# Packed attention and two MLPs: another order and pace for the weight conversions of the first batch

## The chip, the cores and the metric

The kernel runs on one core of a Trainium2 chip. The core's engines each take their own instructions strictly in order and wait for one another through semaphores: PE (TensorE: matrix products and transposes), DVE (VectorE), ACT (ScalarE), POOL (GpSimd) and SP (SyncE, which here only issues transfers between DRAM and on-chip memory). PEld in the profile is PE's loading of weights. The metric is the device time of one execution in microseconds (us); less is better.

## The reference, cut to what matters

For 8 batches of 576 tokens with 8 heads of 64, packed attention is followed by two MLPs on 4608 tokens of 512 features, with 2048 hidden features:

```python
def sm_attn(qq, kk, vv):                    # softmax attention, scale 1/sqrt(64)
    ...
p_packed = sm_attn(p, k, v)                 # 32 packed queries a head
out = sm_attn(q, p_packed, p_packed)
x = out.transpose(0, 2, 1, 3).reshape(B * S, H * D)
h = x @ moe_w_in;  g = h - tanh(h);  x = g @ moe_w_out            # first MLP
h = x @ moe2_w_in; g = s * relu(h) ** 2 + b; out = g @ moe2_w_out  # second MLP
```

The four weight matrices arrive as 64-bit floats; q, k, v and p as 32-bit floats.

## The kernel before, in words

Two stages follow each other. The first goes through the batches and makes attention and the first MLP together; the second makes the second MLP from the result, which lies in DRAM (x2t). Only the start of the first stage is changed.

**Conversion.** `to_f32` makes a 32-bit float of the two 32-bit words of each 64-bit number, in five steps: the absolute value of the high word on ACT (line 118), a clamp (L120), a shift with a mask (L122) and two bitwise merges (L125, L128), the last four on DVE. w_in1 is converted in four quarters of columns, `("w1", c, i)` being half i of quarter c (tiles `w1s_c_i`, result `w1_c`). w_out1 is converted in 16 tiles of 128 rows (`wo1s_j`); each is then split into a high and a low part, `wo[j]`, by ACT (L137) and POOL (L139), since each product is made as three products of such parts.

**The first MLP.** The attention's second product and w_in1 are merged: for each batch and quarter, `make_z` multiplies the packed values with `w1[c]` (`zp`, L364) and splits the result into `z` (L429 on ACT, L431 on DVE). A tile j of 128 hidden features of half a batch (288 tokens, `hf`) is then `mm1` (six products into `h`, L450), `act1` (tanh on ACT, L458; h minus tanh on DVE, L459), `split_g` (`gh` on ACT, L133; `gl` on POOL in batch 0, L134) and, two or three tiles later, `mm2` (twelve products into four banks `acc`, L473). Only two banks hold an `h`, so the third tile's `mm1` waits until the first has passed L459.

**Batch 0** has four parts of eight tiles: both halves with tiles 0 to 7, and then both with tiles 8 to 15 (`part[0]` counts them). Tiles 0 to 7 need quarters 0 and 1 and tiles 0 to 7 of w_out1, tiles 8 to 15 the others. At the end of a part the banks `acc` are emptied into `xs` (L97 on ACT, L99 on DVE) and stored to x2t (L491); the third and fourth part load this back (L496) and add it (L485).

**What sets the order.** The program is written out by hand through generators. `fill` is a list of steps beside the tiles: the conversions and the attention of this and the next batch. In batch 0 `AFTER[part]` steps are put behind each `mm1`, and `SLOTS[part]` sixths of a step at each of a tile's six slots; `until(key, fill)` forces as many as a product still needs. Within `first_weights`, `in_turn` takes groups one after the other, the members of a group by turns (`both`), and gives each member of the next group its first step early. `CATCH_UP` steps follow each `mm1` once the weights are done, until the first half of batch 1 has its attention. Each engine then runs what this leaves in its queue.

**Places.** Half quarters of w_in1 are loaded into nine slots, in the order of `turns`. The 64-bit tiles 0 to 7 of w_out1 lie in places of `wo` that are filled last; tiles 8 to 11 and 13 can only be loaded when POOL has split one of those, tile 12 lies in `cv`. All these loads, the store of `xs` and the loads of q, k, v and p (L168, L175, L176, L226, L237) are in SP's one queue, in program order.

Of the kernel before, what the change touches and what calls it, by code (L numbers as in the profile page):

```python
# [18 lines left out]
def pack_attention_two_mlps(ctx, tc, q, k, v, p, w_in1, w_out1, w_in2, w_out2, s_in, b_in, out):  # L19
# [33 lines left out]
    LAND = 14  # L53
    W_K, W_P, W_PK, W_PV, W_E, W_Q = 2, 9, 5, 1, 7, 3

    AFTER, SLOTS = (3, 4, 1, 1), (0, 1, 4, 1)
    AHEAD, CATCH_UP, FIRST_W = 13, 11, (23, 25, 26, 27, 28)
    EXP_LO, EXP_HI = 2.0 ** -15, 2.0 ** 16 * 1.875
    assert 2 * R == P and NB == 2 * C and 4 * M == P and 2 * D == P and H * D == DM

# [460 lines left out]
    def run(g):  # L521
        for _ in g:
            pass

    with tc.manual_schedule():
# [72 lines left out]
        def second_stage(b, hf):  # L598
            yield from scores2(b, hf)
            yield from both([stage2(b, hf, g) for g in range(G)])  # L600
            done.add(("a", b, hf))

        def in_turn(*groups):

            groups = [[call_late(g) for g in group] for group in groups]
            for n, group in enumerate(groups):
                for i, _ in enumerate(both(group)):
                    yield
                    if i == min(AHEAD, 4 * len(group)) and n + 1 < len(groups):
                        for g in groups[n + 1]:  # L610
                            next(g)

        def call_late(f):
            g, *a = f
            yield from g(*a)
# [14 lines left out]
        v_t[0, 0] = v_t[0, 1] = first_rows(v[0], P, v_0, flat(wslot(F32, "v_0_1")))  # L630
        q_t[0, 0] = first_rows(q[0, :, :HB], QT, wo_place(4), odd[:, :DM])
        take_turn()
        load_wo1(0, 1)
        q_t[0, 1] = first_rows(q[0, :, HB:], QT, wo_place(6), wo_place(7))
        load_wo1(2, 3)
        take_turn()
        take_turn()
        load_wo1(4, 5, 6, 7)
        make_identity(nc, ident)
        nc.vector.memset(mask, 0.0)  # L640
        nc.vector.memset(ones, 1.0)
# [11 lines left out]
                next(conv, None)  # L653
        free(len(own) + 1)
        run(conv)
        rest = in_turn([(wo1_steps, 0), (wo1_steps, 1)], [(wo1_steps, 2), (wo1_steps, 3)])
        run(both([second_stage(0, 0), first_z(0), seq(wait(10), turn_q(1))]))
        nc.sync.dma_start(out=s_sb, in_=s_in.partition_broadcast(P))
        nc.sync.dma_start(out=b_sb, in_=b_in.partition_broadcast(P))

        def first_weights():
            yield from rest
            yield from in_turn(
                [(w1_steps, 1, 0), (w1_steps, 1, 1)],
                [(first_z, 1), (wo1_steps, 4), (wo1_steps, 5), (second_stage, 0, 1)],
                [(wo1_steps, 6), (wo1_steps, 7)],
                [(w1_steps, 2, 0), (w1_steps, 2, 1)],
                [(first_z, 2), (wo1_steps, 8), (wo1_steps, 9)],
                [(wo1_steps, 10), (wo1_steps, 11)],
                [(w1_steps, 3, 0), (w1_steps, 3, 1)],  # L670
                [(first_z, 3), (wo1_steps, 12), (wo1_steps, 13)],
                [(wo1_steps, 14), (wo1_steps, 15)])

        pend = []

# [74 lines left out]
        def attention():  # L750

            yield from first_weights()
            load_p(1)
            load_k(1, 0)
            load_v(1, 0)
            for b in range(B):
                if b:
                    for c in range(2, NCH):
                        yield from make_zs(b, c)
                    yield from second_stage(b, 1)  # L760
                if b + 1 == B:
                    return
                load_q(b + 1, 0)
                if b + 2 < B:
                    load_p(b + 2)
                nxt = (b + 2, 0) if b + 2 < B else None
                yield from step_p(b + 1)
                yield from stage1(b + 1, 0, (b + 1, 1), (b + 1, 1))
                yield from stage1(b + 1, 1, nxt, nxt)
                if b:  # L770
                    for c in range(2):
                        yield from make_zs(b + 1, c)
                    yield from second_stage(b + 1, 0)
                else:
                    yield from both([seq(make_zs(1, 0), make_zs(1, 1)), second_stage(1, 0)])
                load_q(b + 1, 1)
# [501 lines left out]
```

## Time and profile before

| | |
|---|---|
| median of 3 runs | 1574.1 us (1573.82 to 1574.97) |
| profiled execution | 1574.41 us |
| its span, first to last instruction | 1572.3 us |
| PE busy | 1485.0 us, 94% of the span |
| DVE busy | 1087.2 us, 69% |
| ACT busy | 745.7 us, 47% |
| POOL busy | 114.5 us, 7% |
| mean granted TensorE clock | 0.973 |

A share of busy time is a mean over stages with different limits, so the stretches of the first 210 us are to be looked at by themselves. The granted clock is 1.0 at the higher of two levels (2.4 GHz) and 0.5 at the lower (1.2 GHz); a stretch with both lies between. A wait in a row is put down to the instruction that ended it last.

### The profile page before, as it was taken

How to read it: one execution, taken by the hardware profiler on the slowest of the kernel's cores; microseconds unless marked ns; L12 is line 12 of the kernel's file. 1: busy time of each engine (PE TensorE's matmuls, PEld its weight loads, DVE VectorE, ACT ScalarE, POOL GpSimd, SP SyncE). 2: the span in 40 equal slices, each digit the busy share in tenths (PEclk: the TensorE clock that was granted, in tenths of full speed). 3: DMA queues.
4: the chain of work that ended last, by engine and by line, in shares of the span. 5: the costliest groups of instructions: out<-in, count | busy, mean ns of one | idle time of the engine just before them, and what ended most of it. 6: DMA issues, size and time to landing. Idle time of an engine off the chain costs nothing.

```text
span 1572.3 us, 27031 instructions
## 1 busy us (share of the span) xinstructions
PE 1485.0 (94%) x10020; PEld 1392.0 (89%) x10020; DVE 1087.2 (69%) x2074; ACT 745.7 (47%) x1433; POOL 114.5 (7%) x143
## 2 busy tenths in 40 slices
PE   5576899999999999999999999999998999999998
PEld 3365688888889889989999999999998999999998
DVE  5777686868769687786744677677676865566563
ACT  3343344444444444443433566566566664454452
POOL 0324200000000010101102000000022000000000
PEclk8588999999999999999999999999999999999999
DMA  9544736464554626352524664664679886686683
GB/s 234 146 115 106 144 82 152 114 151 112 126 139 113 150 77 146 89 132 79 170 82 183 238 251 171 232 240 180 233 270 332 270 255 195 209 254 190 210 243 81
DMA packets 373652, 271.02 MB, mean 172 GB/s; under 512 B 238096, under 2 KB 321040, under 8 KB 373520
## 3 DMA queue, kind: packets, MB, share of 16 engines
q1 hardware_dynamic: 366720, 246.69, 53.2%
q0 software_dynamic: 6272, 22.02, 4.0%
q8 instruction: 78, 1.28, 0.3%
q10 hardware_dynamic: 528, 0.59, 0.1%
q14 instruction: 54, 0.44, 0.1%
HBM read 161.09 MB, written 108.13 MB: 171 GB/s over the span
## 4 chain that ended last, share of the span: by engine, by line
PE 78%; DVE 9%; DMA 4%; SPq 3%; issue 3%; ACT 2%; POOL 0%; ACTq 0%; DVEq 0%; POOLq 0%
PE acc L473 19%; PE Y L1216 10%; PE h L450 9%; PE Y L999 9%; PE Z L1216 6%; PE X L999 6%; PE X L1216 6%; PE Z L999 6%; PE zp L364 2%; DMA w1s<-in_moe_w_in_dram 2%; PE pv L338 1%; PE s L268 1%; SPq L192 1%; DVE gl L134 1%; DVE t L459 1%
## 5 line engine op out<-in xcount | busy, mean ns | idle before, releaser
L473 PE MATMUL acc<-gh,wo 128*128 128x288 f32 x2040 | 422.9, 298 | 1.3 <-POOL wo L139 1.3
L473 PEld LDWEIGHTS acc<-gh,wo 128*128 128x128 f32 x2040 | 333.5, 191 | 1.9 <-POOL wo L139 1.9
L473 PE MATMUL acc<-gl,wo 128*128 128x288 f32 x1020 | 314.6, 308 | 11.8 <-POOL gl L134 8.2
L458 ACT ACTIVATE t<-h 128x288 f32<-128x288 f32 x256 | 105.1, 411 | 333.7 <-PE h L450 287.3
L473 PEld LDWEIGHTS acc<-gl,wo 128*128 128x128 f32 x1020 | 194.5, 191 | 51.7 <-issue 37.2
L459 DVE TENSOR_TENSOR t<-h,t 128x288 f32<-128x288 f32 x256 | 116.2, 454 | 177.6 <-ACT t L458 176.5
L450 PE MATMUL h<-a2h,z 128*128 128x288 f32 x1024 | 216.5, 299 | 3.7 <-DVE z L431 3.7
L903 DVE TENSOR_TENSOR x<-B,x 128x768 fp32r<-128x768 f32 x158 | 147.3, 951 | 80.1 <-ACT x L1150 67.1
L450 PEld LDWEIGHTS h<-a2h,z 128*128 128x128 f32 x1024 | 167.5, 192 | 4.2 <-DVE z L431 4.2
L999 PE MATMUL Y<-x,w 128*128 128x384 f32 x864 | 160.6, 339 | 4.8 <-DVE g L903 4.0
L450 PE MATMUL h<-a2l,z 128*128 128x288 f32 x512 | 155.6, 304 | 7.5 <-DVE a2l L415 6.4
L999 PEld LDWEIGHTS Y<-x,w 128*128 128x128 f32 x864 | 152.9, 190 | 5.4 <-DVE g L903 4.4
L1216 PE MATMUL Y<-x,w 128*128 128x384 f32 x864 | 153.2, 335 | 0.7 <-DVE s L903 0.7
L1216 PEld LDWEIGHTS Y<-x,w 128*128 128x128 f32 x864 | 150.3, 188 | 1.0 <-DVE s L903 1.0
L1150 ACT CAST x<-B 128x768 fp32r<-128x768 f32 x116 | 94.1, 834 | 45.0 <-DMA B<-g 24.4
L450 PEld LDWEIGHTS h<-a2l,z 128*128 128x128 f32 x512 | 98.7, 193 | 13.1 <-DVE a2l L415 7.0
L133 ACT CAST gh<-t 128x288 fp32r<-128x288 f32 x255 | 108.6, 426 | 0.0
L999 PE MATMUL X<-x,w 128*128 128x384 f32 x576 | 108.0, 336 | 0.0
L999 PE MATMUL Z<-x,w 128*128 128x384 f32 x576 | 107.9, 336 | 0.0
L134 DVE TENSOR_TENSOR gl<-t,gh 128x288 fp32r<-128x288 f32 x224 | 104.0, 464 | 0.0
L1216 PE MATMUL X<-x,w 128*128 128x384 f32 x576 | 102.9, 337 | 0.0
L1216 PE MATMUL Z<-x,w 128*128 128x384 f32 x576 | 102.0, 335 | 0.0
(164 smaller groups left out, 2061.7 us busy)
## 6 DMA issues: line engine op xcount, KB each, us to landing
g<-g SPq DMA_DIRECT2D x196, 384.0 KB, 3.6
B<-g SPq DMA_DIRECT2D x116, 384.0 KB, 4.6
w<-w_d POOLq DMA_DIRECT2D x28, 512.0 KB, 5.3
B<-x2t SPq DMA_DIRECT2D x24, 384.0 KB, 5.8
g<-s SPq DMA_DIRECT2D x24, 384.0 KB, 2.9
out_dram<-g SPq DMA_DIRECT2D x192, 48.0 KB, 1.8
x2t<-xs SPq DMA_DIRECT2D x15, 576.0 KB, 3.5
w1s<-in_moe_w_in_dram SPq DMA_DIRECT2D x32, 256.0 KB, 8.0
```

The lines of the kernel that those rows point to most:

```text
L133: nc.scalar.copy(hi, x)
L134: (eng or nc.vector).tensor_tensor(out=lo, in0=x, in1=hi.bitcast(F32), op=ALU.subtract)
L192: nc.sync.dma_start(out=t.rearrange("p (h d) -> p h d", h=H), in_=src[:, t0:t0 + m].rearrange("h p d -> p h d"))
L364: nc.tensor.matmul(ps[e][i * M:(i + 1) * M, :rhs(i).shape[-1]], pblk[b][r, h // 4, h % 4 * M:h % 4 * M + M], rhs(i)[r], start=True, stop=True)
L450: nc.tensor.matmul(h[:, :HB], zt[:, zi, g, f0:f0 + P], a[:, g], start=(n == 0), stop=(n == 3 * G - 1))
L458: nc.scalar.activation(t, h[:, :HB], AF.Tanh)
L459: nc.vector.tensor_tensor(out=t, in0=h[:, :HB], in1=t, op=ALU.subtract)
L473: nc.tensor.matmul(acc[m][:, :HB], w[:, m * P:(m + 1) * P], x, start=(j == js[0] and i == 0), stop=(j == js[-1] and i == 2))
L903: self.nc.vector.tensor_tensor(out=o, in0=a, in1=b, op=op)
L999: self.nc.tensor.matmul(bank[:, f, :self.TH], w[:, f, a, kt], x[:, b, kt], start=(p in ("P1", "P5", "P6") and m == 0), stop=(m == 5), skip ...
L1150: self.nc.scalar.copy(self.xs[(7 * self.NBK + n) % self.XS][:, 0], self.ready[0])
L1216: nc.tensor.matmul(bank[:, ft, :T], w[:, kk, u, ft], x[:, v, kk], start=first and p in ("P1", "P5", "P6"), stop=last, skip_group_check=True)
```

## The change

The order of the groups in `first_weights` is new. Each quarter of w_in1 is converted one half after the other, as two groups of their own, with one or two groups of w_out1 tiles behind them, before the group that holds its product `first_z`; the groups that stood ahead of it (`rest`) are gone. The pace is new: AFTER and SLOTS are (6, 5, 4, 1) and (5, 3, 4, 1) instead of (3, 4, 1, 1) and (0, 1, 4, 1), CATCH_UP is 4 instead of 11. The loads of w_out1 tiles 0 to 7 stand together behind both halves of the second quarter of w_in1 and q's second half. The first loads of batch 1 (`second_loads`) are now part of a group in `first_weights` instead of following all of it.

```diff
@@ -53,8 +53,8 @@
     LAND = 14
     W_K, W_P, W_PK, W_PV, W_E, W_Q = 2, 9, 5, 1, 7, 3
 
-    AFTER, SLOTS = (3, 4, 1, 1), (0, 1, 4, 1)
-    AHEAD, CATCH_UP, FIRST_W = 13, 11, (23, 25, 26, 27, 28)
+    AFTER, SLOTS = (6, 5, 4, 1), (5, 3, 4, 1)
+    AHEAD, CATCH_UP, FIRST_W = 13, 4, (23, 25, 26, 27, 28)
     EXP_LO, EXP_HI = 2.0 ** -15, 2.0 ** 16 * 1.875
     assert 2 * R == P and NB == 2 * C and 4 * M == P and 2 * D == P and H * D == DM
 
@@ -600,6 +600,11 @@
             yield from both([stage2(b, hf, g) for g in range(G)])
             done.add(("a", b, hf))
 
+        def second_loads():
+            for f, *a in ((load_p, 1), (load_k, 1, 0), (load_v, 1, 0), (load_q, 1, 0)):
+                f(*a)
+                yield
+
         def in_turn(*groups):
 
             groups = [[call_late(g) for g in group] for group in groups]
@@ -630,12 +635,10 @@
         v_t[0, 0] = v_t[0, 1] = first_rows(v[0], P, v_0, flat(wslot(F32, "v_0_1")))
         q_t[0, 0] = first_rows(q[0, :, :HB], QT, wo_place(4), odd[:, :DM])
         take_turn()
-        load_wo1(0, 1)
         q_t[0, 1] = first_rows(q[0, :, HB:], QT, wo_place(6), wo_place(7))
-        load_wo1(2, 3)
         take_turn()
         take_turn()
-        load_wo1(4, 5, 6, 7)
+        load_wo1(0, 1, 2, 3, 4, 5, 6, 7)
         make_identity(nc, ident)
         nc.vector.memset(mask, 0.0)
         nc.vector.memset(ones, 1.0)
@@ -653,23 +656,23 @@
                 next(conv, None)
         free(len(own) + 1)
         run(conv)
-        rest = in_turn([(wo1_steps, 0), (wo1_steps, 1)], [(wo1_steps, 2), (wo1_steps, 3)])
         run(both([second_stage(0, 0), first_z(0), seq(wait(10), turn_q(1))]))
         nc.sync.dma_start(out=s_sb, in_=s_in.partition_broadcast(P))
         nc.sync.dma_start(out=b_sb, in_=b_in.partition_broadcast(P))
 
         def first_weights():
-            yield from rest
             yield from in_turn(
-                [(w1_steps, 1, 0), (w1_steps, 1, 1)],
-                [(first_z, 1), (wo1_steps, 4), (wo1_steps, 5), (second_stage, 0, 1)],
-                [(wo1_steps, 6), (wo1_steps, 7)],
-                [(w1_steps, 2, 0), (w1_steps, 2, 1)],
-                [(first_z, 2), (wo1_steps, 8), (wo1_steps, 9)],
-                [(wo1_steps, 10), (wo1_steps, 11)],
-                [(w1_steps, 3, 0), (w1_steps, 3, 1)],
-                [(first_z, 3), (wo1_steps, 12), (wo1_steps, 13)],
-                [(wo1_steps, 14), (wo1_steps, 15)])
+                [(w1_steps, 1, 0)], [(w1_steps, 1, 1)],
+                [(wo1_steps, 0), (wo1_steps, 1)],
+                [(first_z, 1), (wo1_steps, 2), (wo1_steps, 3)],
+                [(wo1_steps, 4), (wo1_steps, 5)],
+                [(second_stage, 0, 1), (wo1_steps, 6), (wo1_steps, 7)],
+                [(w1_steps, 2, 0)], [(w1_steps, 2, 1)],
+                [(wo1_steps, 8), (wo1_steps, 9)],
+                [(first_z, 2), (wo1_steps, 10), (wo1_steps, 11), (second_loads,)],
+                [(w1_steps, 3, 0)], [(w1_steps, 3, 1)],
+                [(wo1_steps, 12), (wo1_steps, 13)],
+                [(first_z, 3), (wo1_steps, 14), (wo1_steps, 15)])
 
         pend = []
 
@@ -750,9 +753,6 @@
         def attention():
 
             yield from first_weights()
-            load_p(1)
-            load_k(1, 0)
-            load_v(1, 0)
             for b in range(B):
                 if b:
                     for c in range(2, NCH):
@@ -760,7 +760,8 @@
                     yield from second_stage(b, 1)
                 if b + 1 == B:
                     return
-                load_q(b + 1, 0)
+                if b:
+                    load_q(b + 1, 0)
                 if b + 2 < B:
                     load_p(b + 2)
                 nxt = (b + 2, 0) if b + 2 < B else None
```

In the rows of the built program below, `t_0_9` is the `t` of half 0, tile 9 (a last number is the buffer's); a `t` of 128x512 with no such numbers is a w_out1 tile under conversion.

First place: DVE, at the first two tiles of the first part. Before, from the first L459 on:

```order
L459 TENSOR_TENSOR t_0_0_482<-h_0_0_470,t_0_0_482 128x288
L120 TENSOR_SCALAR t_479<-t_479 128x512
L122 TENSOR_SCALAR t_477<-t_477 128x512
L122 TENSOR_SCALAR t_479<-t_479 128x512
L459 TENSOR_TENSOR t_0_1_495<-h_0_1_485,t_0_1_495 128x288
L125 SCALAR_TENSOR_TENSOR t_477<-wo1s_174,t_477 128x512
L125 SCALAR_TENSOR_TENSOR t_479<-wo1s_176,t_479 128x512
```

and now:

```order
L122 TENSOR_SCALAR w_1_179<-w_1_179 128x1024
L125 SCALAR_TENSOR_TENSOR w_1_179<-w1s_0_180,w_1_179 128x1024
L128 SCALAR_TENSOR_TENSOR w_1_179<-w1s_0_180,w_1_179 128x1024
L120 TENSOR_SCALAR w_1_179<-w_1_179 128x1024
L459 TENSOR_TENSOR t_0_0_484<-h_0_0_470,t_0_0_484 128x288
L122 TENSOR_SCALAR w_1_179<-w_1_179 128x1024
L125 SCALAR_TENSOR_TENSOR w_1_179<-w1s_1_185,w_1_179 128x1024
L128 SCALAR_TENSOR_TENSOR w_1_179<-w1s_1_185,w_1_179 128x1024
L120 TENSOR_SCALAR t_497<-t_497 128x512
L120 TENSOR_SCALAR t_499<-t_499 128x512
L122 TENSOR_SCALAR t_497<-t_497 128x512
L459 TENSOR_TENSOR t_0_1_504<-h_0_1_488,t_0_1_504 128x288
```

The second quarter (`w_1`) has moved from behind four w_out1 tiles to ahead of all of them, and there are more conversion rows to each L459.

Second place: DVE, where the conversions end (`wo1s_1176` before and `wo1s_1092` now hold tiles 14 and 15 of w_out1). Before:

```order
L459 TENSOR_TENSOR t_0_13_1291<-h_0_13_1282,t_0_13_1291 128x288
L128 SCALAR_TENSOR_TENSOR wo1s_1176<-wo1s_1176,t_1240 128x512
L125 SCALAR_TENSOR_TENSOR t_1266<-wo1s_1176,t_1266 128x512
L128 SCALAR_TENSOR_TENSOR wo1s_1176<-wo1s_1176,t_1266 128x512
L459 TENSOR_TENSOR t_0_14_1323<-h_0_14_1314,t_0_14_1323 128x288
```

and now:

```order
L459 TENSOR_TENSOR t_0_8_1185<-h_0_8_1173,t_0_8_1185 128x288
L122 TENSOR_SCALAR t_1167<-t_1167 128x512
L128 SCALAR_TENSOR_TENSOR wo1s_1092<-wo1s_1092,t_1167 128x512
L125 SCALAR_TENSOR_TENSOR t_1167<-wo1s_1092,t_1167 128x512
L431 TENSOR_TENSOR z_3_1130<-zp_3_1_1132,z_3_1130 128x512
L128 SCALAR_TENSOR_TENSOR wo1s_1092<-wo1s_1092,t_1167 128x512
L459 TENSOR_TENSOR t_0_9_1220<-h_0_9_1207,t_0_9_1220 128x288
```

The last conversion has moved from the L459 of tile 14 to that of tile 9 of the third part.

Third place: SP's queue, from the last of w_out1 tiles 8 to 11 on (`w1s_0`, `w1s_1` are the two halves of the fourth quarter, `cv` is w_out1 tile 12, the row behind it tile 13, the L550 row tiles 14 and 15). Before:

```order
L568 DMA wo1s_813<-in_moe_w_out_dram 128x512
L491 DMA x2t<-xs_0_859 512x1x288
L147 DMA w1s_0_875<-in_moe_w_in_dram 32x2x512 x4
L147 DMA w1s_1_880<-in_moe_w_in_dram 32x2x512 x4
L568 DMA cv<-in_moe_w_out_dram 128x512
L568 DMA wo1s_1115<-in_moe_w_out_dram 128x512
L491 DMA x2t<-xs_1_1152 512x1x288
L496 DMA xp_0_1158<-x2t 128x4x288
L550 DMA wo1s_1176<-in_moe_w_out_dram 128x2x512
L226 DMA pc_1342<-in_p_dram 128x2x64
L168 DMA k_0_0_1344<-in_k_dram 32x18x32 x4
L168 DMA k_0_1_1349<-in_k_dram 32x18x32 x4
```

and now:

```order
L147 DMA w1s_0_812<-in_moe_w_in_dram 32x2x512 x4
L147 DMA w1s_1_852<-in_moe_w_in_dram 32x2x512 x4
L491 DMA x2t<-xs_0_884 512x1x288
L226 DMA pc_914<-in_p_dram 128x2x64
L168 DMA k_0_0_941<-in_k_dram 32x18x32 x4
L168 DMA k_0_1_946<-in_k_dram 32x18x32 x4
L175 DMA v_0_961<-in_v_dram 64x4x320
L176 DMA v_0_961<-in_v_dram 64x4x256
L237 DMA q_0_0_0_986<-in_q_dram 32x9x32 x4
...
L568 DMA cv<-in_moe_w_out_dram 128x512
L568 DMA wo1s_1051<-in_moe_w_out_dram 128x512
L550 DMA wo1s_1092<-in_moe_w_out_dram 128x2x512
```

The fourth quarter has moved ahead of the store of the first part, and batch 1's first loads ahead of w_out1 tile 12.

## Rows read from the trace of the kernel before

**Rows 1.** The page, span in 40 slices: PE's busy tenths, and its granted clock.

```profile
PE   5576899999999999999999999999998999999998
...
PEclk8588999999999999999999999999999999999999
```

**Rows 2.** Busy time by stretch: us, engines (x instructions), PEclk, DMA share, GB/s.

```profile
core 0: us, PE busy (x) PEld busy (x) DVE busy (x) ACT busy (x) POOL busy (x), PEclk, DMA share, GB/s
39.20:161.40 122.20, 77.41 (x459) 65.28 (x459) 91.45 (x140) 47.17 (x96) 44.21 (x37) 0.76 0.48 121
161.40:210.10 48.70, 43.37 (x361) 32.58 (x360) 32.94 (x86) 19.29 (x58) 9.76 (x12) 1.00 0.56 112
```

**Rows 3.** PE's waits, 39.2 to 161.4 us: total us, times, longest us.

```profile
PE zp L364 <- DVE w L128: 19.9, 3, 10.2
```

**Rows 4.** The same stretch, DVE alone, one query each: L120, L122, L125, L128.

```profile
39.20:161.40 122.20, 15.49 (x22) 0.76 0.48 121
...
39.20:161.40 122.20, 17.29 (x22) 0.76 0.48 121
...
39.20:161.40 122.20, 21.43 (x22) 0.76 0.48 121
...
39.20:161.40 122.20, 20.56 (x22) 0.76 0.48 121
```

**Rows 5.** DVE's waits, 39.2 to 161.4 us.

```profile
DVE t L459 <- ACT t L458: 23.1, 10, 4.6
...
DVE w L128 <- PE zp L364: 2.1, 1, 2.1
```

**Rows 6.** Timeline of DVE, last conversion: start us, us, form, idle before.

```profile
159.70 1.69 DVE L128 SCALAR_TENSOR_TENSOR wo1s<-wo1s,t 128x512 int32<-128x512 int32 x1
161.31 0.45 DVE L459 TENSOR_TENSOR t<-h,t 128x288 f32<-128x288 f32 x1
```

**Rows 7.** Chain that ended last, one tile in the first part: start us, us.

```profile
81.39 0.79 PE h L450 x6
82.18 1.61 PE acc L473 x12
```

**Rows 8.** DVE's groups, 39.2 to 161.4 us: busy us, mean ns, idle before.

```profile
L459 DVE TENSOR_TENSOR t<-h,t 128x288 f32<-128x288 f32 x23 | 10.4, 452 | 23.2 <-ACT t L458 23.1
...
L99 DVE COPY xs<-acc 128x288 f32<-128x288 f32 x4 | 1.6, 444 | 0.0
```

**Rows 9.** Tile wo1s, 39.2 to 161.4 us: ns minimum/median/maximum, first and last start.

```profile
L125 DVE SCALAR_TENSOR_TENSOR t<-wo1s,t x15: 676/684/1301, 43.3 to 158.4; 128x512 int32<-128x512 int32 x15
...
L139 POOL TENSOR_TENSOR wo<-wo1s,wo x14: 1287/1482/1841, 47.1 to 159.2; 128x512 fp32r<-128x512 f32 x14
...
DMA to landing us min/median/max: 3.4/3.7/10.2
```

**Rows 10.** Timeline of DVE, conversion rows without POOL beside them.

```profile
41.83 0.42 DVE L120 TENSOR_SCALAR t<-t 128x512 f32<-128x512 f32 x1
...
96.37 0.69 DVE L120 TENSOR_SCALAR w<-w 128x1024 f32<-128x1024 f32 x1 [0.18 <-ACT w L118]
...
99.29 1.21 DVE L125 SCALAR_TENSOR_TENSOR w<-w1s,w 128x1024 int32<-128x1024 int32 x1
```

**Rows 11.** Tile gl, 39.2 to 161.4 us.

```profile
L134 POOL TENSOR_TENSOR gl<-t,gh x22: 794/1037/1359, 43.3 to 160.8; 128x288 fp32r<-128x288 f32 x22
```

**Rows 12.** Timeline of DVE, three of the ten waits of L459.

```profile
80.31 0.46 DVE L459 TENSOR_TENSOR t<-h,t 128x288 f32<-128x288 f32 x1 [1.60 <-ACT t L458]
...
111.41 0.46 DVE L459 TENSOR_TENSOR t<-h,t 128x288 f32<-128x288 f32 x1 [4.65 <-ACT t L458]
...
146.21 0.46 DVE L459 TENSOR_TENSOR t<-h,t 128x288 f32<-128x288 f32 x1 [4.45 <-ACT t L458]
```

**Rows 13.** Timeline of SP's issues: start us, us to the last of them.

```profile
144.30 7.93 SPq L168 DMA_DIRECT2D k<-in_k_dram  x8
...
153.62 8.69 SPq L237 DMA_DIRECT2D q<-in_q_dram  x16
```

## The prediction

> **What bounds the kernel now.** I read the 40 slices of the page first: the reader is to see that PE is at 9 tenths from the sixth slice on, and that the hole is in the first five, some 196 us, where its granted clock is low too [rows 1]. The table by stretches gives it a size. From the first h product (39.2 us) to the last conversion of a weight tile on DVE (161.4 us) PE works 77.4 of 122.2 us at a mean clock of 0.76, and DVE 91.45; from there to the third tile of the second batch (210.1 us) PE works 43.4 of 48.7 us at full clock [rows 2]. What the change can win lies in the 122.2 us. What comes after 210.1 us should only move as a whole: PE's instructions stand there in the same order as before (but for two tiny column sums), and PE is full.
>
> PE's waits in that stretch say why: 19.9 us in three waits for zp, the product that turns a quarter of w_in1 into z, behind L128, the last step of that quarter's conversion [rows 3]. DVE is the engine waited for, and it is not full itself: 122.2 − 91.45 = 30.8 us idle. Most of its work there is conversion, L120, L122, L125 and L128 with 74.8 us together [rows 4]. Of its idle time 23.1 us, in ten waits, is L459 (h minus tanh) waiting for the tanh [rows 5], which in turn waits for an h that PE could not yet make. So the two wait for each other by turns: DVE stands at an L459 because little conversion is put ahead of it, and PE stands at a zp whose quarter is not yet converted.
>
> **The point where no time is won.** Before, the last L128 ends at 161.4 us, and the next L459 is that of tile 14 of the third part [rows 6]. In the changed order the last L128 stands ahead of the L459 of tile 9 (second place shown of the order). PE so has five tiles more to do after the last conversion. One tile at full clock is six products for h, 0.79 us, and twelve for acc, 1.61 us [rows 7]: 5 × 2.40 = 12.0 us. The change wins by as much as the last conversion comes earlier than 161.4 − 12.0 = **149.4 us**, if the stretch behind it runs as it does now.
>
> **DVE's work up to there.** No conversion is added or removed. Of the 23 L459, 17 are left ahead of the last L128 (6 × 0.452 = 2.7 us less), and of the four L99 on DVE that empty acc two (0.9 us less) [rows 8]; they move behind it, where DVE works 32.9 of 48.7 us and hides them [rows 2]. That leaves 91.45 − 3.6 = 87.9 us.
>
> This holds time that DVE loses to POOL. Undisturbed, L125 on a tile of w_out1 takes 0.68 us, its minimum [rows 9] (L128 alike) and L120 0.42 (L122 alike); on half a quarter of w_in1 L120 takes 0.69 and L125 1.21 (L122 and L128 alike) [rows 10]. Sixteen tiles at 2 × (0.42 + 0.68) = 2.2 us and six halves at 2 × (0.69 + 1.21) = 3.8 us make 58.0 us; 74.8 were measured, 16.8 more. POOL's own work, at its minima, is 15 × 1.29 for wo and 22 × 0.79 for gl, 36.7 us [rows 9, 11]. So DVE loses 0.46 us for each of POOL, about the share of the stretch in which DVE has conversion to do (58.0 of 122.2, 0.47). In a stretch of about 99 us that share is 0.59; POOL has five gl fewer ahead of the last L128, 32.8 us, so the loss is 19.4 us, 2.6 more than now. DVE's work: **90.5 us**.
>
> The Trainium skill ("SBUF — State Buffer", section "Who interferes with whom") says that GpSimd and VectorE take turns at one port pair under an exclusive lock, the later one blocking fully. The mean of 0.46 does not contradict it, since DVE is often not there to be blocked; by the rule alone each us of POOL in a stretch full of conversion would cost DVE one, and that is the fourth rival.
>
> **DVE's idle time up to there.** The two waits of L459 at the zp of the third and fourth quarter, 4.65 and 4.45 us [rows 12], go, and the 2.1 us at L128 [rows 5], since each quarter is now converted a group ahead of its product. Four waits like that of 1.60 us [rows 12] come in tiles 4 to 7 of the first part, where no conversion stands between two L459; now four or five rows of it do, and these 6 us go as well. Of 30.8 us that leaves some 13. Of these I take off 6, for waits that now find a conversion ahead of them in the queue (about 11 steps a tile in the first part), and add 2 for one new wait, next: **9 us**. The bounds are nothing and the old 30.8.
>
> **Transfers on SP's queue.** The second_loads put p, k, v and q of batch 1 (27 transfers) ahead of tile 12 of w_out1, which lands in cv (third place of the order). Before, k to q were issued from 144.30 to 162.31 us, in 18.0 us [rows 13]. Now they stand behind the store of the first part, which waits for L99. In the sum below, L99 comes at about 99 us: 138.7 less 13 for tiles 10 to 15, 8 for the fourth quarter, 6 for z and L459, 8 lost to POOL and 5 idle. With 1 for the store and p, 18.0, and 3.4 to 3.7 to land [rows 9], tile 12 is there at 121 to 122 us. DVE comes to it at 121 (138.7 less 9 for four tiles, 3 for z and L459, 4 lost to POOL, 2 idle). That is a wait of 0 to 3 us, in which the tanh of tile 6 is queued on ACT behind that tile's L118. The loads of the fourth quarter stand ahead of that store now, which costs nothing. Tiles 0 to 3 of w_out1 land later, but are wanted later too, behind two halves of the second quarter (7.6 us of DVE). CATCH_UP at 4 for 11 costs nothing while PE is busy anyway; without that cover I price it at the 5.3 us for which PE is idle after 161.4 us [rows 2].
>
> **The sum.** 39.2 + 90.5 + 9 = 138.7 us for the last conversion, 149.4 − 138.7 = 10.7 us won. The profiled execution took 1574.41 us, 0.3 above the median of the runs (its span is 1572.3, with 2.1 around it): 1574.4 − 10.7 = **1563.7 us**, rounded to 1564. Bounds: with no idle time and the old loss to POOL 39.2 + 87.9 = 127.1, 22.3 us won, and if five more tiles of cover hide PE's 5.3 us too, 27.6: 1547. With the old idle time 39.2 + 90.5 + 30.8 = 160.5, 11.1 us lost: 1585.
>
> **Rivals.** (1) DVE hardly waits: 1547 to 1556. For it: each L459 now has two to eight conversion rows ahead of it, so its tanh can be done when it comes up. Against: the chain from h over tanh, gh and gl to acc takes several instructions on four engines, and PE is at its low clock there [rows 1].
> (2) SP's queue is the new bound. If each of the 27 transfers takes 1.0 us, as the eight k did (7.93 us) [rows 13], tile 12 comes 9 us later, and the tanh held on ACT lets nothing past: 10.7 − 9 = 1.7 us won, 1573, no change. Against: the sixteen q took 0.54 us each [rows 13].
> (3) Slower. The tanh stands on ACT behind L137, which waits for DVE's L128, and L459 stands on DVE behind more conversion, so that the two wait for each other once a tile and PE falls to its low clock. At the old mean of 2.3 us a wait (23.1 / 10), 17 tiles make 39 us idle: the last conversion at 168.7, 19.3 us lost, 1594; with the old 30.8, 1585. It decides from 149.4 − 39.2 − 90.5 = 19.7 us idle on, 1.2 us a tile. For it: this is how L459 waits today [rows 5]. Against: the longest of those waits end in a wait for zp, which the order takes away.
> (4) POOL costs DVE its whole 32.8 us, 13.4 more than I take: 152.1 us, 2.7 lost, 1577, no change. Against: the 0.46 measured.
> By the skill's rule the fourth would follow; the measured mean bears against it only as long as DVE has gaps.
>
> **How the numbers follow.** Forecast, 1556 to 1571: 0.58. Rival 1: 0.17. Rival 2: 0.10. Rival 3: 0.10. Rival 4: 0.05. A difference of 0.2%, 3.1 us, is about what a measurement of this kernel can tell from no change. Faster by more than that are the forecast, rival 1 and the mild third of rival 2: 0.78. Slower by more is rival 3: 0.10. The rest, 0.12, is within it. The time is that of the forecast. The range leaves out rival 3, the last us of rival 4 and the lower edge of rival 1: 1549 to 1576.
>
> **What the profile after would show.** Right: the last L128 of a w_out1 tile on DVE at 132 to 146 us, with DVE idle for under 15 us from 39.2 us on; PE's waits at zp for L128 down from 19.9 to a few us; the third tile of the second batch at about 199 us, and all later stretches as long as before. The SP step is right if cv's load is issued at about 118 us and its L118 waits for under 4 us. Wrong: waits of L459 of 20 us in all (rival 3), 8 us or more at L118 for cv (rival 2), conversion rows at over 1.5 times their minimum (rival 4), or PE idle for well over 5 us after the last L128: then the gain was given back in the stretch that I took over unchanged.

## The result, and the profile after

The changed kernel takes 1559.6 us (median of 4 runs, 1558.9 to 1560.8), the kernel before 1574.5 us on the same chip: a ratio of 0.991 [0.989, 0.992], faster by 14.9 us, which is well over the 0.2% that can be told from no change. Its profiled execution took 1560.75 us with a span of 1558.8, against 1574.41 and 1572.3; the spans differ by 13.5 us, and the traces are compared on that.

The page's slices of PE and of its granted clock answer to [rows 1]. The hole is still in the first five, but shorter:

```profile
PE   5768999999999999999999999999998999999998
...
PEclk7698999999999999999999999999999999999999
```

The table by stretches answers to [rows 2]: from the first h to the end of the last L128 of a w_out1 tile, and from there to the third tile of the second batch.

```profile
39.90:136.20 96.30, 66.38 (x360) 55.18 (x361) 86.86 (x133) 41.79 (x85) 36.54 (x32) 0.77 0.57 149
136.20:195.50 59.30, 56.83 (x460) 45.84 (x460) 39.25 (x100) 25.39 (x72) 13.45 (x17) 1.00 0.56 124
```

The first stretch fell from 122.2 to 96.3 us, although DVE works only 4.6 us less in it: its idle time fell from 30.8 to 9.4 us. PE's clock in it is no better (0.77 for 0.76). The four conversion lines, which answer to [rows 4], stand in the same order (L120, L122, L125, L128) and have the same 22 rows each:

```profile
39.90:136.20 96.30, 15.93 (x22) 0.77 0.57 149
...
39.90:136.20 96.30, 14.54 (x22) 0.77 0.57 149
...
39.90:136.20 96.30, 20.61 (x22) 0.77 0.57 149
...
39.90:136.20 96.30, 19.84 (x22) 0.77 0.57 149
```

Together 70.9 us, where 74.8 were measured before. The waits of PE in that stretch, beside [rows 3], and those of DVE, beside [rows 5]:

```profile
PE acc L473 <- POOL gl L134: 14.4, 6, 4.3
...
PE zp L364 <- DVE w L128: 2.6, 2, 1.7
```

The first of them read so in the kernel before:

```profile
PE acc L473 <- POOL gl L134: 8.2, 4, 3.3
```

```profile
DVE t L459 <- ACT t L458: 4.3, 4, 1.6
DVE t L120 <- ACT t L118: 3.5, 3, 2.4
```

PE's 19.9 us at zp are down to 2.6, but its waits for gl, 8.2 us before, are now 14.4. The longest shows what is behind such a wait. On ACT the gh of the tile (L133) stands behind an L137, which had waited 4.84 us for a conversion on DVE; gl is made from that gh, and PE waited 4.35 us for gl:

```profile
68.42 0.69 ACT L137 CAST wo<-wo1s 128x512 fp32r<-128x512 f32 x1 [4.84 <-DVE wo1s L128]
...
70.98 0.41 ACT L133 CAST gh<-t 128x288 fp32r<-128x288 f32 x1
...
72.22 0.97 POOL L134 TENSOR_TENSOR gl<-t,gh 128x288 fp32r<-128x288 f32 x1
...
73.24 0.61 PE L473 MATMUL acc<-gl,wo 128*128 128x288 f32 x1 [4.35 <-POOL gl L134]
```

So PE still waits for DVE's work there, only at another tile. DVE's 23.1 us at L459 are down to 4.3. The last conversion, beside [rows 6], and DVE's rows at the tile in cv, which is waited for now:

```profile
120.88 0.43 DVE L120 TENSOR_SCALAR t<-t 128x512 f32<-128x512 f32 x1 [2.39 <-ACT t L118]
122.12 0.43 DVE L120 TENSOR_SCALAR t<-t 128x512 f32<-128x512 f32 x1 [0.81 <-ACT t L118]
...
134.65 1.51 DVE L128 SCALAR_TENSOR_TENSOR wo1s<-wo1s,t 128x512 int32<-128x512 int32 x1
136.08 0.44 DVE L459 TENSOR_TENSOR t<-h,t 128x288 f32<-128x288 f32 x1
```

SP's issues up to that tile, beside [rows 13]:

```profile
100.07 6.11 SPq L168 DMA_DIRECT2D k<-in_k_dram  x8
...
107.61 8.71 SPq L237 DMA_DIRECT2D q<-in_q_dram  x16
116.37 0.45 SPq L568 DMA_DIRECT2D cv<-in_moe_w_out_dram  x1
```

For the experiments one more landmark is of use, the last L485 of the first batch (an acc added to the part stored before; behind the colon stand ns min/median/max, then the first and the last start). After, and then before:

```profile
L485 DVE TENSOR_TENSOR xp<-acc,xp x8: 420/442/460, 163.9 to 197.6; 128x288 f32<-128x288 f32 x8
```

```profile
L485 DVE TENSOR_TENSOR xp<-acc,xp x8: 421/446/449, 174.8 to 212.3; 128x288 f32<-128x288 f32 x8
```

So the 13.5 us come about like this: the last L128 is 25.2 us earlier (161.4 to 136.2), the way from it to that L485 is 10.5 us longer (50.9 to 61.4, since five more tiles lie in it), and 1.2 us are given back later (1360.0 to 1361.2 us from there to the end). The time to the last L128 counts from the start of the span; the first h stands at 39.2 us before and at 39.9 after.

### The profile page after: what moved, and what is told of

It reads as the page before. It is cut to its first block, busy times and chain, and to the rows that moved or that the text cites. A ratio compares the mean times of both kernels' runs of the same rounds, so it can differ in the third digit from the quotient of the medians.

```text
span 1558.8 us, 27032 instructions
## 1 busy us (share of the span) xinstructions
PE 1487.8 (95%) x10020; PEld 1395.5 (90%) x10020; DVE 1085.2 (70%) x2074; ACT 745.6 (48%) x1433; POOL 110.5 (7%) x143
## 4 chain that ended last, share of the span: by engine, by line
PE 78%; DVE 11%; SPq 3%; DMA 3%; issue 2%; ACT 2%; POOL 0%; ACTq 0%; DVEq 0%; POOLq 0%
PE acc L473 19%; PE Y L1217 10%; PE h L450 9%; PE Y L1000 9%; PE Z L1217 6%; PE X L1000 6%; PE X L1217 6%; PE Z L1000 6%; PE zp L364 2%; PE pv L338 1%; PE s L268 1%; DVE gl L134 1%; DVE t L459 1%; SPq L192 1%; SPq L237 1%
## 5 line engine op out<-in xcount | busy, mean ns | idle before, releaser
L473 PE MATMUL acc<-gl,wo 128*128 128x288 f32 x1020 | 316.0, 310 | 19.7 <-POOL gl L134 14.4
L459 DVE TENSOR_TENSOR t<-h,t 128x288 f32<-128x288 f32 x256 | 116.2, 454 | 168.7 <-ACT t L458 167.1
L133 ACT CAST gh<-t 128x288 fp32r<-128x288 f32 x255 | 108.5, 426 | 2.3 <-DVE t L459 2.3
```

Of the source, the lines that this page charges most:

```text
L133: nc.scalar.copy(hi, x)
L459: nc.vector.tensor_tensor(out=t, in0=h[:, :HB], in1=t, op=ALU.subtract)
L473: nc.tensor.matmul(acc[m][:, :HB], w[:, m * P:(m + 1) * P], x, start=(j == js[0] and i == 0), stop=(j == js[-1] and i == 2))
```

## The experiments

Twelve more runs were made, eleven kernels and the changed one once more, all timed against the kernel before. In the table "L128" is the end of the last one on a w_out1 tile, "tail" the way from it to the last L485, "tiles" how many more (or fewer) tiles than in the changed kernel lie in that tail, all from one profiled execution of each; "won" is the median against that of the kernel before in the same comparison (1574.6, 1574.2 or 1575.3 us).

| kernel | us | ratio, 95% | won | L128 | tail | tiles |
|---|---|---|---|---|---|---|
| before | 1574.5 | | | 161.4 | 50.9 | -5 |
| changed | 1559.6 | 0.991 [0.989, 0.992] | 14.9 | 136.2 | 61.4 | 0 |
| changed_again | 1559.8 | 0.989 [0.988, 0.991] | 15.5 | 136.5 | 61.3 | 0 |
| pace_alone | 1567.9 | 0.995 [0.994, 0.997] | 6.8 | 138.6 | 67.4 | 0 |
| order_alone | 1564.8 | 0.994 [0.993, 0.995] | 9.8 | 144.2 | 56.1 | -3 |
| old_groups | 1564.2 | 0.994 [0.993, 0.995] | 10.0 | 139.4 | 62.9 | 0 |
| catch_11 | 1565.9 | 0.995 [0.993, 0.996] | 8.3 | 136.0 | 65.2 | 0 |
| catch_alone | 1580.3 | 1.003 [1.002, 1.004] | -4.9 | 161.6 | 52.3 | -5 |
| pool_more | 1574.7 | 1.000 [0.999, 1.001] | 0.0 | 148.8 | 62.3 | 0 |
| wo_on_dve | 1562.5 | 0.992 [0.991, 0.994] | 11.7 | 134.0 | 65.9 | 0 |
| cv_early | 1556.9 | 0.989 [0.988, 0.991] | 17.8 | 133.9 | 61.2 | 0 |
| loads_behind | 1556.1 | 0.989 [0.987, 0.990] | 18.1 | 133.8 | 62.5 | 0 |
| behind_faster | 1560.2 | 0.991 [0.989, 0.992] | 15.2 | 129.7 | 69.2 | +3 |
| behind_catch_3 | 1554.2 | 0.987 [0.986, 0.988] | 21.2 | 133.2 | 61.4 | 0 |

**Pace and order apart.** My theory at first was that the two need each other; the rival that the pace is everything. The pace alone, in the kernel before:

```diff
-    AFTER, SLOTS = (3, 4, 1, 1), (0, 1, 4, 1)
+    AFTER, SLOTS = (6, 5, 4, 1), (5, 3, 4, 1)
```

> The kernel before with the new AFTER and SLOTS alone; the groups stand in the old order, all loads are in their old places. My account (the two changes need each other): the three waits of the tensor engine at zp behind L128 stay, because each quarter still stands right ahead of its product; they may be shorter, but at 10 us or more in all (19.9 before), and 2 to 6 us are won, 1568 to 1572 us. Rival (more conversion steps a tile is all there is in the change): the waits of DVE at L459 fall to under 10 us, the last L128 ends by 138 us and 12 us or more are won, under 1563 us.

And the changed kernel with that line undone, so with the new order, CATCH_UP and loads (the new order by itself was not run):

> The changed kernel with the old AFTER and SLOTS; the groups, the loads and CATCH_UP are the new ones. The last L128 of a w_out1 tile then stands ahead of the L459 of tile 12 of the third part, three tiles later than in the changed kernel. My account: the waits at zp are gone (under 5 us in all), but with four rows a tile in the first part DVE stands at L459 again, and each tile of cover that is lost costs up to 2.4 us: 1564 to 1571 us, between the two kernels. Rival (the pace is all there is): no better than before, 1573 to 1576 us. Rival (the order is all there is): 1559 to 1561 us.

Each half alone is faster than the kernel before; 1564.8 us for the order lies in the range of my account, 1567.9 for the pace at the edge of it. PE's waits at zp and DVE's at L459 with the pace alone:

```profile
PE zp L364 <- DVE w L128: 23.6, 3, 10.0
...
DVE t L459 <- ACT t L458: 4.9, 6, 1.6
```

and with the order alone:

```profile
PE zp L364 <- DVE w L128: 5.0, 2, 4.1
...
DVE t L459 <- ACT t L458: 11.7, 7, 6.0
```

The stretch up to the last L128 with the pace alone, with the order alone, and in the kernel of the next experiment:

```profile
40.03:138.56 98.53, 61.76 (x370) 50.95 (x370) 83.91 (x133) 41.39 (x82) 38.02 (x31) 0.76 0.57 142
```

```profile
39.72:144.16 104.44, 70.55 (x411) 60.87 (x411) 89.38 (x137) 44.49 (x90) 41.52 (x34) 0.78 0.58 151
```

```profile
41.00:139.35 98.35, 61.56 (x361) 50.19 (x362) 82.68 (x132) 41.76 (x82) 36.27 (x31) 0.76 0.55 146
```

The pace alone takes DVE's waits at L459 away (23.1 to 4.9 us) and brings the last L128 to 138.6 us, while PE waits at zp longer than ever. So that PE stands at zp does not by itself make DVE stand at L459, against my theory. The order alone takes half of those waits away too (11.7 us are left). By all of DVE's idle time either one removes about half: 30.8 us before, 14.6 with the pace, 15.1 with the order, 9.4 with both. The rival is half right: the L128 comes about as early as it said, but only 6.8 of its 12 us are won, because the tail is 6.0 us longer than the changed kernel's. To see whether the old order is what makes it long, the changed kernel was run with the groups alone in the old order:

```diff
-                [(w1_steps, 1, 0)], [(w1_steps, 1, 1)],
-                [(wo1_steps, 0), (wo1_steps, 1)],
-                [(first_z, 1), (wo1_steps, 2), (wo1_steps, 3)],
+                [(wo1_steps, 0), (wo1_steps, 1)], [(wo1_steps, 2), (wo1_steps, 3)],
+                [(w1_steps, 1, 0), (w1_steps, 1, 1)],
...
```

> The changed kernel with the groups of first_weights in the old order; the new AFTER, SLOTS, CATCH_UP, the loads of w_out1 and the second_loads stay. The new pace alone had its last L128 at 138.6 us, though the tensor engine still waited 23.6 us at zp. Account A (the order saves nothing by itself: DVE's work sets the end, and the new pace alone lost its gain behind the last L128, for want of CATCH_UP and second_loads): the last L128 at 136 to 140 us, the waits at zp at 20 us or more, the time 1559 to 1562.5 us. Account B (the waits at zp cost the tensor engine time that it never gets back): 1565 to 1569 us, as with the new pace alone.

```profile
PE zp L364 <- DVE w L128: 24.3, 3, 9.5
```

1564.2 us lies between the two accounts. The waits at zp are all back, but the kernel is only 4.6 us slower than the changed one, and 1.1 us of that is its later first h (41.0 for 39.9 us). Most of the wait at zp is time in which PE would have stood somewhere else: its waits for gl are 10.3 us here, for 14.4. The tail is 62.9 us, so the old order accounts for 1.5 of those 6.0 us at most. What is left of the difference between this kernel and the pace alone are CATCH_UP and where the loads stand.

**CATCH_UP.**

```diff
-    AHEAD, CATCH_UP, FIRST_W = 13, 4, (23, 25, 26, 27, 28)
+    AHEAD, CATCH_UP, FIRST_W = 13, 11, (23, 25, 26, 27, 28)
```

> The changed kernel with CATCH_UP at 11. As predicted (CATCH_UP costs nothing while the tensor engine is busy): 1559 to 1561 us. Rival (with 11 steps a tile the attention of batch 1 comes three to four tiles too early behind the last L128, and the tensor engine stands at products whose inputs are not there, as in the 67.4 us from the last L128 to the last xp with the new pace alone against 61.4 us): 1563 to 1566 us, with the last L128 where it was, at 136 us, and the last xp at 201 us or later.

The prediction's step fell: 11 costs 6.2 us by the medians. The profiled execution was the fastest of its five (1562.66 us) and shows less: its tail is 3.8 us longer, its span 2.1. The last L128 stands where it did, so what the trace shows is lost behind it, where PE is idle for 6.5 of 65.2 us, against 2.5 of 61.4. The first row is this kernel's, the second the changed kernel's:

```profile
135.95:201.20 65.25, 58.73 (x467) 46.70 (x467) 42.11 (x107) 25.71 (x73) 15.28 (x17) 1.00 0.49 113
```

```profile
136.16:197.60 61.44, 58.97 (x475) 47.98 (x475) 41.39 (x105) 25.81 (x73) 13.49 (x17) 1.00 0.54 120
```

Its timeline of PE shows waits in the attention of batch 1 which the changed kernel, with more tile work between two such steps, doesn't have: PE's transpose of the exponentials (e1Tp) stands behind the exponential on ACT, 2.1 us in two waits, and the scores behind kT on DVE, 0.8 us. Another 1.8 us are a wait of acc for an L485:

```profile
142.73 0.66 PE L317 MATMUL e1Tp<-ident,e 128*128 128x128 f32 x4 [1.05 <-ACT e L310]
150.25 1.42 PE L268 MATMUL s<-kT,ppT 128*64 128x288 f32 x6 [0.78 <-DVE kT L288]
```

The same edit (4 for 11) in the kernel before:

> The kernel before with CATCH_UP at 4 for 11, nothing else. In the changed kernel 11 cost 6.2 us, all of it behind the last L128. Account A (the same holds in any kernel, since the steps of batch 1's attention come too early at 11): of the 5.3 us for which the tensor engine is idle behind 161.4 us most are won, 1569 to 1571.5 us. Account B (the price is there only where the attention has a long way to go behind the last L128; before it had only four tiles of that cover, and at 4 steps a tile the z of batch 1 come too late for its tiles): no change or slower, 1573 to 1578 us.

There it costs 4.9 us, more than account B allowed: it has five tiles less behind the last conversion, and at four steps a tile the attention of batch 1 isn't done when the second batch begins. PE waits at its first h, and its granted clock falls to 0.50 there:

```profile
202.93 0.61 PE L450 MATMUL h<-a2l,z 128*128 128x288 f32 x1 [3.07 <-DVE a2l L415]
```

```profile
200.00:205.00 5.00, 2.07 (x8) 2.07 (x9) 3.04 (x11) 0.95 (x3) 0.00 (x0) 0.50 0.00 0
205.00:210.00 5.00, 5.00 (x29) 2.92 (x29) 3.85 (x9) 2.42 (x7) 0.00 (x0) 0.68 0.01 2
```

So 4 is better than 11 with 15 tiles of the first batch left, and 11 better than 4 with ten. Of the 6.0 us by which the tail was too long with the pace alone, CATCH_UP accounts for 3.8 (65.2 less 61.4).

**GpSimd's price.** The low part of each w_out1 tile written twice by GpSimd, with the same values:

```diff
         wo[j] = (t[:, 0], t[:, 1])
+        if eng is nc.gpsimd:
+            yield from split_seq(t[:, 0], t[:, 1], x, eng)
+            eng.tensor_tensor(out=t[:, 1], in0=x, in1=t[:, 0].bitcast(F32), op=ALU.subtract)
+            return
```

> The changed kernel, in which GpSimd writes the low part of each w_out1 tile twice with the same values (13 more rows of 1.3 to 1.5 us, some 17 to 19 us, up to the last conversion on DVE). It separates the price of GpSimd's work to DVE. My account (DVE's work sets the end, and loses about 0.4 us for each us of GpSimd, as 12.9 of 32.8 us in the changed kernel): the conversions take 7 to 8 us more and the time is 1566 to 1568 us. Rival (full blocking): 17 us more, 1575 to 1578 us. Rival (GpSimd costs DVE nothing, and the conversions are long for another reason): 1559 to 1561 us.

And the same part given to DVE:

```diff
-            yield from split_wo(j, "wo1", nc.gpsimd, x)
+            yield from split_wo(j, "wo1", nc.vector, x)
```

> The changed kernel with the low part of each w_out1 tile subtracted on DVE in place of GpSimd, which so has 14 rows (some 20 us) less up to the last conversion; DVE gets 14 rows of about 0.68 us, 9.5 us, more. By doubling that work on GpSimd DVE's busy time up to the last L128 rose by 10.7 us for 23.0 us more of GpSimd, 0.47 each. Account A (the same price the other way): 9.5 more, 9.4 less, no change, 1558 to 1562 us. Rival (full blocking: 20 less, 9.5 more): 1549 to 1552 us. Rival (the 10.7 us came from waits and not from blocking): 1567 to 1570 us.

The same stretch, up to the last L128, in the one and in the other:

```profile
40.07:148.77 108.70, 70.46 (x366) 58.34 (x367) 97.51 (x133) 41.90 (x84) 59.47 (x46) 0.70 0.51 132
```

```profile
40.15:133.96 93.81, 64.54 (x370) 53.37 (x370) 85.22 (x147) 41.70 (x84) 15.87 (x17) 0.80 0.58 154
```

Doubling adds 23.0 us to GpSimd (59.5 for 36.5; each row got longer too) and 10.7 to DVE: 0.47 for each us. Taking it away leaves 20.6 us less on GpSimd; DVE's time falls by 1.6 although it does 14 rows of 0.69 us more (9.7), so by 11.3: 0.55. On the conversion rows alone it is 9.1 us more and 9.4 less, 0.39 and 0.46. My size of 7 to 8 us was too small, and so was my time for the whole: 1574.7 us lies next to the rival's 1575. It is DVE's busy time that decides between the two, since full blocking of all GpSimd time would have been 23 and 21 us; the rest of the last L128's 12.6 us is 1.8 us of idle time and a first h 0.1 us later. Single rows do show a full block. With the doubled work two L122 on tiles of w_out1, 0.42 us each when undisturbed (as the L120 in [rows 10]), take 1.47 each, as long as one row of GpSimd, while GpSimd works from 56.12 to 60.46 us without a gap; from the timelines of the two engines:

```profile
56.36 2.94 DVE L122 TENSOR_SCALAR t<-t 128x512 int32<-128x512 int32 x2
```

```profile
56.12 1.47 POOL L139 TENSOR_TENSOR wo<-wo1s,wo 128x512 fp32r<-128x512 f32 x1
57.55 2.91 POOL L155 TENSOR_TENSOR wo<-wo1s,wo 128x512 fp32r<-128x512 f32 x2
```

That agrees with what the Trainium skill ("SBUF — State Buffer", section "Who interferes with whom") says of a row that meets the other engine's: it blocks fully. A row of nine elements shows it best, L398 of the attention. In the changed kernel its two rows meet the low parts on GpSimd; in the kernel that gives these to DVE they take 0.29 us on average:

```profile
L398 DVE TENSOR_SCALAR st<-st 128x9 f32<-128x9 f32 x2 | 2.2, 1082 | 0.0
```

That the mean is lower, about half, because the two often don't meet, fits these rows and was not tested by itself.

The second kernel's last L128 is 2.2 us earlier than the changed kernel's, and yet it is no faster: 2.8 us slower by the medians, though the intervals of the two ratios overlap (account A, no change, is missed by 0.5 us). In its profiled execution, the slowest of its five, the tail is 4.5 us longer. Its last two subtractions stand on DVE ahead of the L99 that empty acc; PE waits 1.62 us for the copy of acc on ACT and 1.82 us for that L99. Its granted clock is 1.00 in the 6 us ahead of these waits and 0.50 in the 6 us behind them. One row of its timeline, and the table by stretches:

```profile
137.56 0.61 PE L473 MATMUL acc<-gl,wo 128*128 128x288 f32 x1 [1.82 <-DVE xs L99]
```

```profile
134.00:137.00 3.00, 0.64 (x3) 0.43 (x3) 3.00 (x5) 2.00 (x5) 1.53 (x2) 0.91 0.00 0
137.00:140.00 3.00, 2.44 (x10) 2.43 (x11) 2.69 (x8) 0.37 (x1) 0.00 (x0) 0.50 0.29 106
140.00:143.00 3.00, 3.00 (x15) 2.24 (x15) 0.46 (x1) 0.73 (x2) 0.14 (x1) 0.50 0.51 103
```

**SP's queue.** Only the load of the tile in cv moved up, out of the way of the 27 transfers:

```diff
             if j in (5, 7):
                 load_wo1(j + 3, j + 4)
+            if j == 7:
+                load_wo1(12)
             if j == 11:
-                load_wo1(12, 13)
+                load_wo1(13)
```

> The changed kernel, with the load of w_out1 tile 12 (the one that goes to cv) issued behind tile 7 in place of behind tile 11, ahead of batch 1's first loads on SP's queue; tile 13 stays. My account: DVE waited 3.2 us at L120 and L118 of cv and of tile 13 in the changed kernel, 2.4 of them for cv; these 2.4 go, unless tile 13 is then waited for instead; the last L128 comes 1 to 3 us earlier and the time is 1556.5 to 1559 us. Rival (the wait only moves to the next L459, whose tanh is not done): 1559 to 1560.5 us.

And the changed kernel without second_loads, its loads where they were before:

```diff
-                [(first_z, 2), (wo1_steps, 10), (wo1_steps, 11), (second_loads,)],
+                [(first_z, 2), (wo1_steps, 10), (wo1_steps, 11)],
...
             yield from first_weights()
+            load_p(1)
+            load_k(1, 0)
+            load_v(1, 0)
...
-                if b:
-                    load_q(b + 1, 0)
+                load_q(b + 1, 0)
```

> The changed kernel without the second_loads: p, k and v of batch 1 are loaded behind all w_out1 tiles, and q behind them, as before; tiles 12 and 13 of w_out1 are issued 18 us earlier. Account A (the loads belong where they are now; what they cost is the 3.2 us wait for cv): the last L128 at 132 to 134 us, but the tensor engine waits for kT or qT behind it, and the time is 1558 to 1563 us. Account B (the loads come early enough in either place): the whole 3.2 us are won, 1556 to 1557.5 us. Account C (they are the reason for the 6 us that the new pace alone lost behind the last L128): 1562 to 1566 us.

By the medians they are 2.7 and 3.6 us below the changed kernel, where DVE waited 3.2 us for cv and tile 13. Neither gain is beyond doubt: the runs of the first spread from 1554.5 to 1561.5 us and its ratio is that of changed_again; by the ratios the second is 1 to 3 us, with intervals that overlap. Nor did the wait go in the first. It moved to tile 13, as the expectation had allowed for, and 1.0 us of the 3.5 at L120 was saved:

```profile
DVE t L120 <- ACT t L118: 2.5, 2, 2.2
```

With the loads behind, 0.7 us of it is left. The second's time lies in the range of account B. What it does show is that second_loads bring nothing on the whole: the tail without them is 62.5 us for 61.4, and the last L128 is 2.4 us earlier. My account C, by which their absence made the tail of the pace alone long, fell.

**Two tries for more,** both from the kernel without second_loads: a faster pace, AFTER (7, 6, 4, 1) and SLOTS (6, 4, 4, 1), and CATCH_UP at 3.

```diff
-    AFTER, SLOTS = (6, 5, 4, 1), (5, 3, 4, 1)
+    AFTER, SLOTS = (7, 6, 4, 1), (6, 4, 4, 1)
```

> The changed kernel without the second_loads (1556.1 us), and with AFTER (7, 6, 4, 1) and SLOTS (6, 4, 4, 1): the last L128 stands ahead of the L459 of tile 6 of the second batch of tiles of the fourth part's row, three tiles earlier in the order than in the changed kernel. Account A (DVE's work sets the end; of its 7.6 us idle that are left, the 5.5 at L459 go in part): the last L128 at 130 to 133 us, the time 1552 to 1555.5 us. Rival (a faster pace only puts conversion ahead of L459 that the tensor engine waits for): 1556 to 1561 us, with more waits of acc for gl and of h.

(The place meant is ahead of tile 6 of the second part.)

```diff
-    AHEAD, CATCH_UP, FIRST_W = 13, 4, (23, 25, 26, 27, 28)
+    AHEAD, CATCH_UP, FIRST_W = 13, 3, (23, 25, 26, 27, 28)
```

> The changed kernel without the second_loads (1556.1 us), and with CATCH_UP at 3: behind the last L128 the tensor engine was idle for 3.6 us in that kernel, 2.1 us by its waits for DVE in the attention. Account A (fewer steps a tile still help): 1553.5 to 1555.5 us. Rival (4 is low enough, and at 3 the z of batch 1 are late): 1556 to 1560 us.

The faster pace brings the last L128 to 129.7 us, 4.1 earlier, but ahead of three more tiles, which take 3 × 2.40 = 7.2 us. By the rule of the prediction it should so lose 3.1 us against the kernel it was made from, which I had not worked out ahead of the run: account A fell. By the ratios (0.9905 and 0.9886) it lost 3.0, with intervals that touch. CATCH_UP at 3 is the fastest kernel of the study: 1554.2 us, 5.6 below the changed kernel on the same chip; against CATCH_UP at 4, in another comparison, it is 1.9 us, less than these runs can tell, though the time lies in the range of account A.

The changed kernel was run beside them:

> The changed kernel once more, on the same chip as the three others: 1558.5 to 1560.5 us by every account. Its first h, at 39.9 us in the first look against 39.2 before, may stand between 39.0 and 41.0 (39.1 to 41.0 in seven kernels with either order of the first loads), since that spread does not follow the order of the loads.

Its first h stood at 40.4 us, and in the twelve kernels it stands between 39.1 and 41.0, at 40.0 with the pace alone, which has the old order of loads. The 0.75 us by which the changed kernel began later is within that spread, and differences of a microsecond between two kernels' last L128 are too.

## Why the prediction was right, step by step

The time was 1564 for 1559.6 measured, and its mechanism held for the most part: DVE's work and idle time up to the last conversion set the time, and the tiles behind it cost about what their rows say. In spans 13.5 us were won for 10.7 predicted: the last L128 came 2.5 us earlier than in the sum (136.2 for 138.7), the tail cost 1.5 us less, and 1.2 us were given back behind it.

- **The point where no time is won.** Five more tiles cost 10.5 us for the 12.0 predicted, and that this is so near is in part luck. PE's work behind the last L128 grew by 13.4 us (45.58 to 58.97), and its idle time there fell by 2.9 (5.3 to 2.5), which the sum had taken over unchanged. The row of the kernel before, to set beside that of the changed kernel in the part on CATCH_UP:

```profile
161.39:212.30 50.91, 45.58 (x378) 34.79 (x377) 35.15 (x92) 19.82 (x59) 9.77 (x12) 1.00 0.54 108
```

From the changed kernel's 61.4 us the rule of 2.40 us a tile gives 49.4 (50.9 measured) for the kernel before, 54.2 (56.1) for the order alone and 68.6 (69.2) for the faster pace. It does not give the tail where PE waits in it: with no tile more or less it was 67.4 with the pace alone, 65.2 with CATCH_UP at 11 and 65.9 with the low parts on DVE.
- **DVE's work: 86.9 us for 90.5.** This is the term that was mis-sized. The conversion rows lost 12.9 us to GpSimd (70.9 less 58.0), and two rows of the attention (L398, L401) took 2.1 us more than before: 15.0 where I took 19.4. I had scaled the price by the share of conversion in the stretch, to 0.59 for each us of GpSimd at its minima. On the conversion rows, which is how the old mean of 0.46 was reckoned, it is 12.9 of 32.8, 0.39. So the price did not rise with that share. The two runs on it gave 0.47 and 0.55 by measured time of all rows.
- **DVE's idle time: 9.4 us for 9.** The size was right, and the reason half shown. I put the two longest waits at L459, 4.65 and 4.45 us, down to PE's waits at zp, and gave them to the order. The order alone does take them down, to 2.15 us at most. But so does the pace alone, to 1.57 at most, with PE's waits at zp still there: more conversion rows ahead of an L459 are enough. Which of the two did it in the changed kernel can't be told apart.
- **SP's queue.** L99 at 97.9 us for 99, cv's load at 116.4 for 118, the wait 3.2 us for 0 to 3. That step was right. It did not see that the loads could just as well have stayed behind, nor that the second part of the wait is for tile 13, whose L118 starts as the tile lands:

```profile
121.43 0.66 ACT L118 ACTIVATE t<-wo1s 128x512 f32<-128x512 f32 x1 [0.58 <-DMA wo1s<-in_moe_w_out_dram]
```

- **CATCH_UP.** "Costs nothing while PE is busy" was wrong, by 6.2 us in the medians. It did not show in the time because the sum took the old tail over unchanged, which the changed kernel keeps only with CATCH_UP at 4.
- **Later stretches.** The third tile of the second batch came at 195.4 us for 199; behind the last L485 1.2 us were given back, which the prediction had as nothing. PE's waits up to the second stage are 1.5 us longer there by their rows (8.1 to 9.6); no experiment was made on it, and the cause stays open.

Of the rivals, the first (DVE hardly waits) did not come about as told, with 9.4 us idle; the second (SP's queue) had its wait but at a third of its size; the third (mutual waits at L459) has 4.3 us where it needed 19.7 of idle time, but a part of its mechanism, a tile's row on ACT behind an L137 that waits for L128, is there on PE's side in the 4.35 us shown above; the fourth (all of GpSimd's time lost to DVE) is refuted as a mean price by the doubled and the removed work.

## What to carry to other kernels

Ask of a long wait whether it ends the stretch or only says where the engine stands: PE's 20 us at zp were worth 4.6 us at most, since PE then waits at other tiles, while DVE's idle time, some 21 us less, is most of the 25.2 us by which its last conversion comes earlier. When the end of one engine's work is moved, count what the other still has to do behind it, in its own rows; that rule sizes the tails of three kernels within 2 us and explains why a still faster pace did not win. A number that paces side work (here CATCH_UP) belongs to the distance it has to cover: 4 for 11 won about 6 us with five more tiles to go, and lost 4.9 without them.

## What was not expected of the hardware

Short stalls of PE went with more loss here than their own length: two waits of 1.62 and 1.82 us, in a stretch of 3 us in which PE worked 0.64 us, were followed by 6 us at a granted clock of 0.50 (the lower level), and a wait of 3.07 us by 5 us at 0.68 (a stretch with both levels). That the stalls brought the clock down is read from the order in time; no run tests it by itself. GpSimd's own rows got longer as well when its work was doubled (1.44 us on average for the first writing of a low part and 1.55 for the second, 1.40 in the changed kernel).
